# The first layer's spatial product as seven block products, with sums formed behind the turning

## The chip, the cores and the metric

The kernel runs on one core of a Trainium2 chip. The core has a matrix engine (TensorE; PE in the profile, with its weight loads as PEld), three elementwise engines (VectorE, DVE; ScalarE, ACT; GpSimd, POOL), and a sequencer (SyncE, SP) whose queue issues all of this kernel's transfers. The metric is the device time of one execution in microseconds (us): the median of several executions.

## The reference, cut to what matters

The program computes two attention layers and two gated MLP layers in turn, on x of 2048 rows (S) by 640 columns (D), and the change concerns the first MLP layer:

```python
z = gelu(layernorm(x) @ w_in)                  # 2048 x 1728
z1, z2 = z[:, :864], layernorm(z[:, 864:])
g = w_sp @ z2 + b_sp[:, None]                  # w_sp is 2048 x 2048: the spatial product
x = x + (z1 * g) @ w_out                       # w_out is 864 x 640
```

Both MLP layers use the same w_sp, w_in and w_out, and both attention layers the same q, k, v and o weights. To keep precision with 16-bit operands, every matrix is split in a high and a low half (float16 each), and a product is three: high by high, high by low, low by high.

## The kernel before, in words

Each layer runs in three stages. Attention (`phase1a`, class `Attention`) writes o to DRAM; `phase1b` makes x1, z1 and z2 for 16 tiles t of 128 rows; and the third stage multiplies by w_sp, gates, and multiplies by w_out.

The third stage of the first layer (`phase2`) goes through the 16 row tiles t of w_sp. The rows of tile t are fetched (`rows`, 1 MB), their largest absolute value gives a power-of-two scale (`scale`: one reduction over 2048 columns and five instructions on one column, DVE), the scaled rows are split into halves (`split`: high on ACT, low on DVE), and both 128x1024 column halves are turned by a DMA transpose into `wt` (from the staging tile `wn`). `product` is 96 matmuls per row tile: 16 blocks of 128 by three half products by two column halves of 432. `gate` adds the bias and multiplies by z1 (ACT, DVE), scales and splits the result, and turns it (`ut`); `tail` multiplies it by w_out, 42 matmuls of 320 columns into the two-bank PSUM tile `yp`, of which there is one. The tail of tile t-1 runs behind product t. `early` normalises the new x rows for the next attention. Three quarters of the turned `wt` are stored to DRAM (`store`, `g.turned`) for the second layer.

The third stage of the second layer (`phase2s`) already uses seven block products, as Winograd's form of Strassen's method does: w_sp and z2 are taken as 2x2 blocks (even and odd row tiles, even and odd column tiles of w_sp; the left and right 432 columns of z2), so that a pair p of row tiles costs 7 block products of 24 matmuls each and not 8. The seven combinations of z2 blocks, `zb[0]` to `zb[6]`, are made by `blocks` in `phase1b` (ACT, DVE and POOL). Of the seven combinations of w_sp, three are read back from `g.turned`, and four (S1 to S4) are formed by DVE from scaled rows (scaled by ACT with the scales that the first layer kept) and then turned.

In the third stages the order on PE, SP, DVE and ACT is the order of the code (`manual_schedule(engines=ALLE)`); only POOL's is left to the scheduler. An engine runs its instructions in that order, and one that waits holds up all behind it.

## Time and profile before

| what | value |
|---|---|
| median of 3 executions | 2226.51 us (2224.16 to 2227.24) |
| profiled execution | 2220.46 us, span 2218.7 us |
| first layer: attention, phase1b, third stage (with the next attention's first units) | 0 to 592, 592 to 784, 784 to about 1190 us |
| second layer: attention, phase1b, third stage | to 1690, 1690 to 1877, 1877 to 2219 us |
| busy over the span | PE 95%, DVE 66%, ACT 53%, POOL 42% |

PE is busy nearly all of the time, so a stage is as long as its matmuls where nothing makes PE wait. A row of the table by stage gives, for each engine, busy us and instructions in that stretch, then the granted TensorE clock, the busy share of the DMA engines and GB/s. A row of the timeline gives start, duration, engine, line, operation and tiles, and in brackets the idle time before it and what ended it. `SPq` rows are the issuing of a transfer, not its landing.

### The profile page before, as it was taken

What the parts mean: (1) busy time and instruction counts of PE and PEld (TensorE: products, weight loads), DVE (VectorE), ACT (ScalarE), POOL (GpSimd) and SP (SyncE); (2) the same over time, 40 slices, a digit from 0 to 9 for tenths busy, and PEclk for the clock granted to TensorE, in tenths of its full rate; (3) what the DMA queues carried; (4) which work ended last, traced back from release to release, by engine and by line L of the source; (5) the groups of instructions that cost most, each with busy time, mean ns of one, the idle gap of its engine ahead of it and who ended that gap; (6) DMA issues with size and microseconds to landing.
All of it is one profiled execution on the core that took longest, in us unless ns stands there. A gap on an engine that the chain in (4) does not pass through costs nothing. (4 is left out here: it accounts for less than half of the span.)

```text
span 2218.7 us, 48917 instructions
## 1 busy us (share of the span) xinstructions
PE 2102.8 (95%) x19917; PEld 1269.7 (57%) x19917; DVE 1466.5 (66%) x2804; ACT 1177.0 (53%) x1415; POOL 934.3 (42%) x625
## 2 busy tenths in 40 slices
PE   4889899999899999999999999999989999999999
PEld 2455565666555555555655556666665555555555
DVE  8678888787654654554445787887776667465455
ACT  3499888887632332221222998888875334223321
POOL 2399988888310101000000888788874223000000
PEclk9999999999999999999999999999999999999999
DMA  5624635356746678977655344344566334977875
GB/s 170 181 71 128 142 98 137 106 138 157 177 122 175 165 197 220 248 201 209 187 136 142 93 110 120 105 114 111 147 186 178 100 107 128 251 197 200 225 209 134
DMA packets 515202, 345.03 MB, mean 156 GB/s; under 512 B 409952, under 2 KB 452960, under 8 KB 510624
## 3 DMA queue, kind: packets, MB, share of 16 engines
q1 hardware_dynamic: 514976, 341.90, 59.0%
q8 instruction: 156, 2.56, 0.5%
q14 instruction: 70, 0.57, 0.1%
HBM read 152.53 MB, written 101.20 MB: 114 GB/s over the span
## 5 line engine op out<-in xcount | busy, mean ns | idle before, releaser
L1431 POOL TENSOR_TENSOR PHL<-P,PHL 128x1024 f16<-128x1024 f32 x310 | 658.8, 2133 | 170.6 <-ACT PHL L1430 121.7
L1412 ACT ACTIVATE P<-es,sc 128x1024 f32<-128x1024 f32 x320 | 356.1, 1113 | 85.0 <-PE es L1376 82.1
L1422 DVE TENSOR_REDUCE mx<-mp 128x2 f32<-128x1024 f32 (+2 forms) x384 | 320.9, 861 | 85.6 <-PE mp L1376 84.6
L1430 ACT CAST PHL<-P 128x1024 f16<-128x1024 f32 x320 | 333.5, 1042 | 6.3
L279 POOL TENSOR_TENSOR lnrs<-lnve,mhalf 128x1 f32<-128x1 f32 x92 | 56.4, 620 | 664.2 <-DVE lnve L278 613.8
L375 PEld LDWEIGHTS <-th 128*128 128x128 f16 x1920 | 187.5, 98 | 164.4 <-DMA th<-xnhl 2.6
L757 PE MATMUL gp<-zh,wt 128*128 128x432 f16 x1024 | 231.3, 346 | 0.0
L757 PEld LDWEIGHTS <-wt 128*128 128x128 f16 x1536 | 150.2, 98 | 129.0
L1465 PEld LDWEIGHTS <-PHL 128*128 128x128 f16 x5120 | 167.0, 96 | 52.4 <-DVE oat L1486 13.8
L543 PEld LDWEIGHTS <-wt 128*128 128x128 f16 x1344 | 131.3, 98 | 113.5 <-DMA wt<-wn 1.0
L1465 PE MATMUL pv<-vs,PHL 128*128 128x41 f16 x5120 | 172.6, 182 | 15.6 <-DVE oat L1486 10.8
L375 PE MATMUL zp<-wi,th 128*128 128x432 f16 x960 | 180.5, 346 | 1.9 <-DMA th<-xnhl 1.3
L1176 PE MATMUL vps<-wvh,xt 128*128 128x320 f16 x640 | 157.3, 305 | 11.3 <-DVE vs L1182 5.8
L1405 PEld LDWEIGHTS <-qk 60*128 60x128 f16 (+1 forms) x2048 | 76.7, 94 | 151.0 <-issue 106.1
L1405 PE MATMUL mp<-qk 60*128 60x512 f16 (+3 forms) x1024 | 127.1, 306 | 30.7 <-DVE mx L1422 24.2
L757 PE MATMUL gp<-zl,wt 128*128 128x432 f16 x512 | 135.4, 346 | 0.0
L1405 PE MATMUL es<-qk 64*128 64x256 f16 (+3 forms) x1024 | 124.1, 299 | 11.4 <-ACT P L1412 8.6
L1232 PE MATMUL qps<-xt,wqh 128*128 128x512 f16 x380 | 121.3, 380 | 0.0
L1208 PE MATMUL yps<-wo,o 128*128 128x320 f16 x720 | 119.8, 303 | 1.2 <-DMA o<-o 1.2
L1176 PEld LDWEIGHTS <-xt 128*128 128x128 f16 x960 | 87.7, 100 | 45.6 <-issue 13.7
L770 DVE TENSOR_TENSOR u<-u,cz 128x864 f32<-128x864 f32 x16 | 16.9, 1059 | 144.2 <-ACT u L768 136.6
L1232 PE MATMUL kps<-xt,wkh 128*128 128x512 f16 x340 | 106.8, 379 | 0.6 <-DVE phl L1273 0.4
(276 smaller groups left out, 3935.5 us busy)
## 6 DMA issues: line engine op xcount, KB each, us to landing
wr<-in_B_w_sp_dram SPq DMA_DIRECT2D x32, 1024.0 KB
qk<-st SPq DMA_DIRECT2D x256, 120.0 KB
z<-z SPq DMA_DIRECT2D x32, 432.0 KB
cz<-z SPq DMA_DIRECT2D x32, 432.0 KB
turned<-wt SPq DMA_DIRECT2D x24, 512.0 KB
wt<-turned SPq DMA_DIRECT2D x24, 512.0 KB
st<-qhl SPq DMA_DIRECT2D x40, 256.0 KB
st<-khl SPq DMA_DIRECT2D x40, 256.0 KB
```

Source lines behind the costliest of these rows:

```text
L375: nc.tensor.matmul(zp[:, n, :FHH], a[:, k, :], b[:, k, c:c + FHH], start=(k == 0 and j == 0), stop=(k == KD - 1 and j == 2))
L543: nc.tensor.matmul(o[:, :FHH], wt[:, x, m, :], zb[b][:, y, m, :], start=start and i == j == 0, stop=i == NP - 1 and j == 2, skip_group_che ...
L757: nc.tensor.matmul(gp[:, n, :FHH], ready[t][:, k % 2, a, k // 2, :], b[:, k, n * FHH:(n + 1) * FHH], start=(i == 0 and j == 0), stop=(i == ...
L1176: nc.tensor.matmul(ps, a[:, k, c], b[:, k, n * 320:(n + 1) * 320], start=(i == 0), stop=(i == 14))
L1208: nc.tensor.matmul(ps, a[:, k, :], b[:, k, c], start=(i == 0), stop=(i == 14))
L1232: nc.tensor.matmul(ps, a[:, k, c], b[:, k, :], start=(i == 0), stop=(i == 14))
L1405: nc.tensor.matmul(out[:, h, o:o + w], a[r, ac], b[r, bc], start=o == 0, stop=False, skip_group_check=True)
L1412: self.last_of["ACT"] = nc.scalar.activation(self.Pf[t], es, AF.Exp, scale=g.esc).ins
L1422: self.last_of["DVE"] = nc.vector.tensor_reduce(mx[:, e, :, i], mp[:, :, o:o + w], AX.X, ALU.max).ins
L1430: nc.scalar.copy(hl[:, 0], P)
L1431: (nc.gpsimd if t < self.T - self.TAIL or t % 2 == 0 else nc.vector).tensor_tensor(hl[:, 1], P, hl[:, 0], ALU.subtract)
L1465: nc.tensor.matmul(pv[:, i, h, 0:PVC - 1], self.P[u][:, x, h, o:o + 128], v[:, j, h0 + h, :], start=first and h == x == 0 and (u, o, i, j) ...
```

## The change

The first layer's third stage is now `phase2f`, and takes the same seven block products per pair of row tiles as the second layer's. `phase1b` makes the seven blocks of z2 in both layers (`whole` is gone). What is different from `phase2s` is how the combinations of w_sp come about: all four quarters of a row pair are scaled, split and turned as before (`split`, `turn`), then POOL adds the turned halves up to float32 again (`back`, into the tiles `f0`, `f1`, `f2`), DVE forms S1 to S4 from these (`mix`), and ACT and DVE split each sum into halves (`high`, `low`) straight into the tile that PE reads. There are two staging tiles `wn` and eight `wt` tiles, reused between the quarters and the sums (`place`). The statistics of `early` and its normalising are two steps now.

The seven blocks need more memory than the two tiles before. So the attention weights q, k, v lie where blocks 0, 3, 4 of z will be, and the turned x where block 1 will be and in the place of w_in's and w_out's halves (`g.w0`); the attention weights are stored to DRAM in the first attention (`g.wkept`), and read again behind the last products of the stage. Therefore the next attention's first units and its values, which stood between products 10 to 15, come after the last product, and the attention's pools are opened there (`nxt.sbuf`, `nxt.psum`). The last two tails stand among those units. The first half of w_in is loaded in the background of attention in both layers.

```diff
+def phase2f(g, w_sp, x1_d, z1_d, zb, out, nxt, rest):
...
+    def place(p, b):
+        tag = {"11": "a", "21": "c", "S2": "c", "12": "d", "S3": "e", "S4": "g", "22": f"x{p % 2}", "S1": f"x{1 - p % 2}"}[b]
+        wt[p, b] = (pt0 if tag in ("a", "x0", "c") else pt1).tile([128, 2, NP, 128], F16, tag="wt" + tag, name="wt")
+        return wt[p, b]
...
+    def back(t, i, tag):
+        if t < NT:
+            o = wt[t // 2, f"{t % 2 + 1}{i + 1}"]
+            f[tag] = pf.tile([128, NP, 128], F32, tag=tag, name=tag)
+            nc.gpsimd.tensor_tensor(f[tag], o[:, 0], o[:, 1], ALU.add)
+
+    def mix(o, a, b, op):
+        nc.vector.tensor_tensor(f[o], f[a], f[b], op)
+
+    def high(p, b, tag):
+        if p < NP:
+            nc.scalar.copy(place(p, b)[:, 0], f[tag])
+
+    def low(p, b, tag):
+        if p < NP:
+            nc.vector.tensor_tensor(wt[p, b][:, 1], f[tag], wt[p, b][:, 0], ALU.subtract)
...
+        product(pa, p, "11", 0)
...
+        split(r0, 0)
+        turn(r0, 0)
+        scaled(v, pa, t)
+        scaled(v1, pa, t + 1)
...
+        split(r1, 1)
...
+        product(pc, p, "S1", 3)
+        turn(r1, 1)
+        store(r0, 0)
...
+        back(r0, 0, "f0")
+        split(r1, 0)
...
+        product(pb, p, "S2", 4)
+        turn(r1, 0)
+        rows(r1 + 2)
+        back(r1, 1, "f2")
+        plus(qq, pb, t, v)
+        plus(u[:, FHH:], pc, t, qq)
+        split(r0, 1)
...
+        store(r1, 1)
+        rows(r0 + 2)
+        if pend:
+            now.append(nxt.early(*tail(*pend.pop(0))))
...
+        product(pa, p, "12", 1, False)
+        turn(r0, 1)
+        back(r1, 0, "f1")
+        scaled(u[:, :FHH], pa, t)
+        if not last:
+            mix("f2", "f1", "f2", ALU.add)
+            mix("f1", "f0", "f1", ALU.subtract)
+            mix("f0", "f2", "f0", ALU.subtract)
+            high(q, "S2", "f0")
+            low(q, "S2", "f0")
...
+        if pend:
+            now = [nxt.early(*tail(*pend.pop(0)))]
...
+        product(pb, p, "S3", 5, False)
+        plus(q1, pb, t + 1, v1)
+        plus(u1[:, FHH:], pc, t + 1, q1)
+        high(q, "S3", "f1")
+        low(q, "S3", "f1")
+        store(r0, 1)
+        back(r0, 1, "f1")
...
+        scale(r1 + 2)
...
+        product(pd, p, "22", 6)
+        high(q, "S1", "f2")
+        plus(u1[:, :FHH], pd, t + 1, q1)
+        low(q, "S1", "f2")
...
+        pend.append((*gate(t + 1, u1, z1[0]), x1[0]))
+        if not last:
+            mix("f1", "f1", "f0", ALU.subtract)
...
+        product(pe, p, "S4", 2)
+        high(q, "S4", "f1")
+        plus(u[:, FHH:], pe, t, u[:, FHH:])
+        low(q, "S4", "f1")
+        pend.append((*gate(t, u, z1[1]), x1[1]))
+        scale(r0 + 2)
...
+    nxt.kept_back = []
+    for m in range(2):
+        for nm in "qk":
+            run(nxt.unit(0, m, {nm: bank("abcd"[2 * m + (nm == "k")])[:, :L]}))
+            if nm == "qk"[m == 0]:
+                tail(*pend.pop(0))
+    sb.close()
+    rest.close()
+    nxt.sbuf()
...
```

Two places show how the order moves. The first is DVE in the middle of the first layer's third stage. In a row, `wn` is the staging tile, `wr` a row tile of w_sp, `xo` or `cx` the new rows of x, `q` and `u` the 432-column pieces of g, `f_` the float32 sums, `wt` the turned tile that PE reads. Before, behind one row tile's scale:

```order
L793 SCALAR_TENSOR_TENSOR xo<-cyp,xs,cx_13308 128x640
L745 SCALAR_TENSOR_TENSOR wn<-wr,wiv,wn 128x1024 x2
L276 BN_STATS lnst<-xo 128x6 x2
L277 BN_AGGR lnmv<-lnst 128x2
L278 TENSOR_SCALAR lnve<-lnmv 128x1
L285 TENSOR_SCALAR xt<-xo,lnmv,lnrs 128x640
L770 TENSOR_TENSOR u<-u,cz_13709 128x864
```

The change, behind the scale of the even row tile of a pair:

```order
L742 SCALAR_TENSOR_TENSOR wn<-wr,wiv,wn 128x1024 x3
L786 SCALAR_TENSOR_TENSOR q<-gb,unt,v 128x432
L786 SCALAR_TENSOR_TENSOR u<-gc,unt,q 128x432
L742 SCALAR_TENSOR_TENSOR wn<-wr,wiv,wn 128x1024
L816 SCALAR_TENSOR_TENSOR cx_13259<-cyp,xs,cx_13259 128x640
L292 BN_STATS lnst<-cx_13259 128x6 x2
L293 BN_AGGR lnmv<-lnst 128x2
L294 TENSOR_SCALAR lnve<-lnmv 128x1
L765 TENSOR_TENSOR f_13439<-f_13529,f_13439 128x1024
L765 TENSOR_TENSOR f_13529<-f_13406,f_13529 128x1024
L765 TENSOR_TENSOR f_13406<-f_13439,f_13406 128x1024
L773 TENSOR_TENSOR wt<-f_13406,wt 128x1024
```

The instruction that empties the tail's PSUM tile (L793 before, L816 now) stood ahead of the splits of the next row tile and now stands behind all four splits of the next pair; the sums follow it.

The second place is SP's queue over the same stretch. Before, for one row tile:

```order
L746 DMA_TRANSPOSE wt<-wn 128x16x128 x2
L763 DMA cz_13709<-z_0_6 128x864
L722 DMA wr<-in_B_w_sp_dram 128x2048
L763 DMA cx_13713<-x_0_6 128x640
L750 DMA turned_0<-wt 128x2048
L750 DMA turned_1<-wt 128x2048
L1133 DMA xn<-xnhl 128x1280
```

The change, for one pair, from the fetches of z1 on:

```order
L790 DMA cz_13332<-z_0_4 128x864
L752 DMA_TRANSPOSE wt<-wn 128x16x128 x2
L756 DMA turned_0<-wt 128x2048
L752 DMA_TRANSPOSE wt<-wn 128x16x128
L717 DMA wr<-in_B_w_sp_dram 128x2048
L756 DMA turned_1<-wt 128x2048
L717 DMA wr<-in_B_w_sp_dram 128x2048
L817 DMA x_3<-cx_13259 128x640
L752 DMA_TRANSPOSE wt<-wn 128x16x128
```

Where both staging tiles of a row tile were filled and turned together, the third and the fourth transpose of a pair now stand apart, each behind a store that waits for an earlier transpose to land, and the staging tile of the third is that of the first.

More of the change, by code (lines that the diff above doesn't have):

```diff
@@ L151, in place, with load @@
         return self.h, self.l
-    def load(self, stage, width=864, tag="wst", keep=True, ahead=0):
+    def load(self, stage, width=D, tags=(), keep=True, ahead=0):
         nc = self.g.nc
@@ L398, in phase1b @@
             th = xn_t(xn)
[L399 to L405 removed]
+        more = other_scales(g, wm, (g.wu,), 6, 0, 0) if first else iter(())
         for i, t in enumerate(ts):
```

517 lines of the change are left out of this document (290 added, 227 removed).

## The prediction

> **What bounds the kernel now.** I read the table by stage first, for the first layer's third stage, two pairs of row tiles inside the third stages of both layers, and the last 67 us of the second layer's phase1b.
>
> ```profile
> 784.00:1206.00 422.00, 417.91 (x2494) 241.72 (x2493) 201.50 (x365) 97.11 (x111) 32.75 (x36) 1.00 0.75 198
> ...
> 875.00:922.00 47.00, 47.00 (x281) 27.27 (x280) 24.34 (x45) 10.54 (x11) 3.90 (x4) 1.00 0.95 252
> ...
> 1962.00:2004.00 42.00, 42.00 (x253) 24.61 (x252) 21.92 (x33) 11.32 (x11) 0.00 (x0) 1.00 0.81 212
> ...
> 1810.00:1840.00 30.00, 29.54 (x164) 15.69 (x162) 21.46 (x38) 14.88 (x18) 9.05 (x9) 1.00 0.40 116
> 1840.00:1877.00 37.00, 36.34 (x200) 19.31 (x199) 27.27 (x48) 13.45 (x20) 12.44 (x12) 1.00 0.45 106
> ```
>
> Columns are PE, PEld, DVE, ACT and POOL busy, clock, DMA share, GB/s. In the third stages PE never idles and DVE (third figure) is busy half of the time. So PE sets the length, and seven products for eight would be worth their matmuls, as long as DVE stays below PE. The timeline gives the sizes: PE of the second layer (a block product of 24 matmuls every 4.38 us), then DVE of the first layer's third stage over one row tile.
>
> ```profile
> 1900.00 4.54 PE L543 MATMUL gd<-zb,wt 128*128 128x432 f16 x24
> ...
> 1904.38 4.54 PE L543 MATMUL ge<-zb,wt 128*128 128x432 f16 x24
> ```
>
> ```profile
> 982.76 1.06 DVE L770 TENSOR_TENSOR u<-u,cz 128x864 f32<-128x864 f32 x1 [8.91 <-ACT u L768]
> ...
> 986.80 1.12 DVE L780 SCALAR_TENSOR_TENSOR un<-u,uiv,un 128x864 f16<-128x864 f32 x1 [1.01 <-ACT un L778]
> 987.83 2.28 DVE L728 TENSOR_REDUCE am<-wr 128x1 f32<-128x2048 f32 x1
> ...
> 990.85 0.88 DVE L793 SCALAR_TENSOR_TENSOR xo<-cyp,xs,cx 128x640 f32<-128x640 f32 x1
> 992.09 2.48 DVE L745 SCALAR_TENSOR_TENSOR wn<-wr,wiv,wn 128x1024 f16<-128x1024 f32 x2 [0.36 <-ACT wn L744]
> 994.49 0.88 DVE L276 BATCH_NORM_STATS2 lnst<-xo 128x6 f32<-128x320 f32 x2
> ...
> 996.46 0.61 DVE L285 TENSOR_SCALAR xt<-xo,lnmv,lnrs 128x640 f32<-128x640 f32 x1 [0.67 <-POOL lnrs L279]
> 1005.99 1.06 DVE L770 TENSOR_TENSOR u<-u,cz 128x864 f32<-128x864 f32 x1 [8.91 <-ACT u L768]
> ```
>
> The period is 1005.99 - 982.76 = 23.23 us; four products are 17.52, so a tail is 5.71. DVE stands idle for 8.91 us of it. From the same rows: a gate holds DVE for 5.07 us (982.76 to 987.83, with 1.01 of waiting for ACT), a scale 3.02 (to 990.85), a tail's last step 0.88, statistics 1.3 (994.49 to the reciprocal root on POOL), normalising 0.61, a low half of a split 1.24.
>
> **The change part by part.** Added on DVE per pair of row tiles are four sums, four low halves of sums, and five additions out of PSUM; on ACT high halves of sums and the smaller first terms. The second layer has them (by line and shape):
>
> ```profile
> L515 DVE TENSOR_TENSOR s<-s,wr 128x1024 f32<-128x1024 f32 x7 | 8.6, 1225 | 5.4 <-ACT wr L499 4.8
> L527 DVE TENSOR_TENSOR wn<-s,wn 128x1024 f16<-128x1024 f32 x14 | 17.0, 1218 | 0.0
> L550 DVE SCALAR_TENSOR_TENSOR q<-gb,unt,v 128x432 f32<-128x432 f32 x16 | 10.6, 662 | 12.0 <-PE gb L543 12.0
> L522 ACT CAST wn<-s 128x1024 f16<-128x1024 f32 x14 | 14.6, 1044 | 47.9 <-DVE s L515 47.9
> L547 ACT ACTIVATE v<-ga,bsp,unt 128x432 f32<-128x432 f32 x16 | 10.4, 697 | 1.2 <-PE ga L543 1.2
> L744 ACT ACTIVATE wn<-wr,wiv 128x1024 f16<-128x1024 f32 x28 | 30.6, 1140 | 41.4 <-DVE wiv L732 41.4
> ```
>
> *Matmuls.* Eight block products fewer: 8 x 4.38 = 35.0 us. A pair costs PE 7 x 4.38 + 2 x 5.71 = 42.1 us instead of 46.5.
>
> *DVE's sum.* Two scales 6.0, four low halves of splits 5.0, four sums 4.9, four low halves of sums 4.9, five additions 3.4, two gates 10.1, two tails with their normalisation 5.6: 39.9 us of PE's 42.1. Nothing is left for waiting, and DVE's queue is strictly in order. So waits decide.
>
> *The turning.* From the issue of a transpose, or the end of DVE's low half right before it, to PE as the waiting reader of the turned tile (timeline, second layer; the third pair of rows under a full DMA queue):
>
> ```profile
> 1817.70 1.65 SPq L293 DMA_TRANSPOSE th<-xnhl  x1
> 1821.72 5.65 PE L375 MATMUL zp<-wi,th 128*128 128x432 f16 x30 [0.46 <-DMA th<-xnhl]
> ```
>
> ```profile
> 2203.88 1.12 DVE L569 SCALAR_TENSOR_TENSOR un<-u,uiv,un 128x864 f16<-128x864 f32 x1 [1.01 <-ACT un L567]
> ...
> 2209.62 3.03 PE L575 MATMUL ga<-w,ut 128*128 128x320 f16 x21 [0.41 <-DMA ut<-un]
> ```
>
> ```profile
> 1886.18 7.36 SPq L536 DMA_TRANSPOSE wt<-wn  x1
> ...
> 1895.61 4.55 PE L543 MATMUL gb<-zb,wt 128*128 128x432 f16 x24 [0.61 <-DMA wt<-wn]
> ```
>
> Ten blocks took 4.0 us, fourteen 4.6, so sixteen about 4.9 (estimate); 9.4 when the queue was full. Between these I take 4.9, since the quarters of one pair are turned one at a time behind light traffic. The Trainium skill, "DMA: Bandwidth & Descriptors", section "Latency and other measured facts", gives DMA transposes 261 GB/s, which makes 512 KB 2.0 us; the sum of the stage would by that be near the third rival's below, about no change. The rows here disagree with it as a landing time: 4.6 us for 448 KB.
>
> *POOL's additions.* The trace has none from two halves; the nearest row has the same size. Below it, POOL and DVE in the second layer's phase1b:
>
> ```profile
> L1431 POOL TENSOR_TENSOR PHL<-P,PHL 128x1024 f16<-128x1024 f32 x310 | 658.8, 2133 | 170.6 <-ACT PHL L1430 121.7
> ```
>
> ```profile
> L446 DVE TENSOR_TENSOR zb<-z,zb 128x432 f16<-128x432 f32 x23 | 26.5, 1177 | 4.3 <-ACT zb L445 4.3
> ...
> L446 DVE TENSOR_TENSOR zb<-zt,zb 128x432 f16<-128x432 f32 x29 | 18.2, 660 | 2.4 <-ACT zb L445 2.3
> ```
>
> I take 2.1 us for one. The second pair shows one and the same DVE form at 660 ns, and at 1177 where POOL subtracts at the time: DVE with two SBUF tensors stands still while POOL works. Bounds for this: 0, and all four additions, 8.5 us per pair.
>
> *One cycle of DVE*, from the end of the even tile's scale. Low half of r0's left quarter at 2.4 (ACT's high half first, 1.14). ACT then has the two first terms (1.4), so the second low half ends at 4.9. The third waits for a staging tile: the first transpose lands at 7.3, ACT takes until 8.4, but POOL's addition has begun at 7.3 and DVE gets through at 9.4; ends 10.7. Two additions, 12.1. POOL's second addition goes first, so the fourth low half ends at 14.1. Now DVE empties the tail: 15.0, statistics 16.3. The third transpose was issued at 10.7, landed at 15.6, was added by 17.7; only then come three sums (21.4), S2's high half on ACT, its low half (23.7), normalising, second tail and statistics (26.5), two additions (27.9), S3's low half and normalising (29.7), a scale (32.7), an addition and S1's low half (34.6), a gate (39.7), a sum, an addition and S4's low half (42.8), a gate (47.9), a scale: **50.9 us**, against 46.5 for a pair before. PE follows: the second tail needs the one PSUM tile that DVE empties at 15.0, so PE's pair ends at 15.0 + 5.7 + 3 x 4.38 = 33.8 in DVE's cycle.
>
> *Sum of the stage.* Its start: in the second layer DVE is done with z2 4.3 us after PE's first product (below), here a scale lies between, 7.3. The first pair has no tails or normalisation (-5.6) but the split of w_out (seven pieces of 0.88, 6.2); S4's sum falls in a wait: DVE ends it at about 58.
>
> ```profile
> 1877.31 4.54 PE L543 MATMUL ga<-zb,wt 128*128 128x432 f16 x24
> ...
> 1879.07 2.54 DVE L446 TENSOR_TENSOR zb<-zt,zb 128x432 f16<-128x432 f32 x3
> ...
> L91 DVE SCALAR_TENSOR_TENSOR wul<-wst,iv,wuh 128x640 f16<-128x640 f32 x6 | 5.2, 884 | 10.5 <-ACT wuh L90 10.5
> ```
>
> Then five cycles (254.5), PE's 33.8 to the end of the seventh pair, a last pair at PE's own 42.1 (nothing is left to prepare), and two tails, 11.4: 399.8. Before: 16 x 23.23 = 371.7. The stage becomes **28 us longer** where PE alone would make it 35 shorter.
>
> *phase1b of the first layer.* Blocks instead of two halves: the second layer's does that with PE hardly waiting. But the preparation behind its last tiles is heavier: in its last 67 us DVE is busy 21.46 + 27.27 = 48.7; the second layer's preparation in it (four sums, two low halves, 7.3) goes, four scales, four low halves, three sums and one more low half (22) come: 63 of 67. I charge 3 us, bounds 0 and 8.
>
> *The end of the stage.* Values and units come later, with no product to hide their ACT and DVE steps, but values now follow the units and hide the trip of q and k through DRAM. Before, PE loses 6.0 us there:
>
> ```profile
> 1180.00:1206.00 26.00, 21.91 (x144) 12.01 (x143) 11.97 (x17) 4.96 (x9) 0.69 (x1) 0.97 0.83 198
> 1206.00:1230.00 24.00, 22.09 (x198) 12.37 (x196) 17.97 (x28) 11.34 (x18) 4.21 (x2) 0.96 0.51 108
> ```
>
> I take no difference, bounds -5 and +6. The weights' extra 10 MB go out and come in where the DMA has room: nothing, for the reload starts three products and more ahead of its reader.
>
> Sum: 28 + 3 = **+31 us**: 2220.5 becomes 2251.5 for the profiled execution, and 2226.5 becomes 2257.5, say 2258, for the median, which lies 6 us above the profile.
>
> **The rivals.**
> - *Landing hidden.* Transposes land in time and POOL blocks nothing; DVE's own order still holds. Then the third and fourth low halves end at 6.2 and 8.9, sums start at 11.1, and a cycle is 44.3. The same sum (first pair, five cycles, PE's offset, last pair with two tails) is 52 + 221.5 + 28.6 + 53.5 = 355.6, 16 less than before; 2213 with phase1b. Faster, and it decides from a cycle of about 45 downwards. Against it: both waits are in the order, with 4.0 us as the shortest landing seen.
> - *PE bound.* DVE runs ahead of PE throughout: -35, 2191. Against it: 39.9 of 42.1 us without one handover to ACT.
> - *Landing in 2.4 us.* From ten to fourteen blocks the landing grew by 0.6 us, which makes 2.4 for sixteen without a fixed part; POOL still blocks. The cycle is then 47.1 and the sum 375: about +3, with phase1b 2232, and no change where POOL blocks little. By the 261 GB/s of the Trainium skill ("DMA: Bandwidth & Descriptors", the same section) the kernel would end here too.
> - *Queue full.* Rows, stores and fetches of z1 lie before the transposes, and a landing takes 7 us (between 4.9 and 9.4): the cycle is 55.1, the stage 425, +53 by the same sum; 2282.
>
> **How the numbers follow.** Forecast 0.60, landing hidden 0.12, PE bound 0.05, landing in 2.4 us 0.08, queue full 0.15. Its own range: landings from 4.0 with nothing blocked (cycle 48.2, stage 381, +10) to 6 us (+44): 2236 to 2272. The range over all reaches to the hidden landing and to the full queue: 2212 to 2288. A difference of 0.2% is 4.5 us, about what this kernel's measurement can tell. Faster: 0.12 + 0.05 and half of the short landing, 0.21; slower: 0.60 + 0.15 less its lower edge, 0.72; same 0.07.
>
> **What would show it.** In the changed kernel's stage DVE busy near 40 us in a pair that lasts about 51; PE idle before the second tail (released by DVE's step that empties PSUM), and DVE idle before the third low half and before the first sum (released by ACT behind a transpose, and by POOL). Rows of the forms above should keep their durations; two-tensor ones on DVE should lengthen beside POOL's additions. I am wrong if PE has no idle time in pairs two to seven, if DVE's cycle is under 46, or if the loss lies in phase1b or at the stage's end instead.

## The result, and the profile of the changed kernel

The changed kernel takes 2290.07 us (median of 4 runs, 2288.22 to 2294.76) where the kernel before takes 2225.34 us beside it: a ratio of 1.0295, 95% interval 1.0274 to 1.0315. It is slower, as forecast, but by 65 us and not by 31. Its profiled execution took 2288.59 us against 2220.46 us, 68.1 us more.

Where they went, by the start times in TensorE's timelines of the two kernels (layer 1 up to the last row):

| stretch | before | after | difference | forecast |
|---|---|---|---|---|
| up to the first product of phase1b | 591.9 | 595.3 | +3.4 | 0 |
| phase1b | 191.8 | 200.2 | +8.4 | +3 (0 to 8) |
| third stage, block products and tails | 371.7 | 423.1 | +51.4 | +28 |
| units, values, up to the first score of layer 2 | 40.4 | 50.9 | +10.5 | 0 (-5 to +6) |
| the rest (layer 2) | | | -5.6 | 0 |

The third stage first. TensorE's timeline of the changed kernel over one pair, from the second tail of one to that of the next; in brackets the time it stood idle and who released it:

```profile
1040.50 8.31 PE L813 MATMUL cyp<-w,ut 128*128 128x320 f16 x42 [6.93 <-DVE cx L816]
1048.65 4.54 PE L779 MATMUL gb<-zb,wt 128*128 128x432 f16 x24
...
1074.93 5.87 PE L813 MATMUL cyp<-w,ut 128*128 128x320 f16 x42
1080.64 4.55 PE L779 MATMUL ga<-zb,wt 128*128 128x432 f16 x24
1092.14 8.09 PE L813 MATMUL cyp<-w,ut 128*128 128x320 f16 x42 [6.96 <-DVE cx L816]
```

The pair lasts 1092.14 - 1040.50 = 51.6 us. The second tail waits 7 us for the step that empties the one PSUM tile, the place the forecast named. And behind such a wait the same 42 matmuls take 8.1 to 8.3 us instead of 5.87. Now DVE and ACT around the first of these waits:

```profile
1034.52 2.07 DVE L742 SCALAR_TENSOR_TENSOR wn<-wr,wiv,wn 128x1024 f16<-128x1024 f32 x1 [3.84 <-ACT wn L741]
1039.57 0.87 DVE L816 SCALAR_TENSOR_TENSOR cx<-cyp,xs,cx 128x640 f32<-128x640 f32 x1
1043.20 3.74 DVE L765 TENSOR_TENSOR f<-f,f 128x1024 f32<-128x1024 f32 x3 [1.41 <-POOL f L762]
```

```profile
1033.34 1.15 ACT L741 ACTIVATE wn<-wr,wiv 128x1024 f16<-128x1024 f32 x1 [3.98 <-DMA wt<-wn]
```

The third low half waits for ACT, ACT for a transpose to leave its staging tile, and the sums wait for POOL: what the forecast laid out. The groups by line for the whole stage, then for phase1b (busy, mean of one, idle time before them and who ended it):

```profile
L813 PE MATMUL cyp<-w,ut 128*128 128x320 f16 (+1 forms) x672 | 109.3, 328 | 53.4 <-DVE cx L816 44.4 <-ACT w L90 4.1 <-DVE w L91 4.0
L779 PE MATMUL gb<-zb,wt 128*128 128x432 f16 x384 | 74.9, 353 | 7.6 <-DVE q L786 7.6
...
L384 PE MATMUL zp<-wi,th 128*128 128x432 f16 x480 | 91.8, 350 | 6.7 <-DMA th<-xnhl 6.7
```

44.4 us in six waits are the second tails. The others stand in the first two pairs (w_out's halves 8.1, q 7.6) and in phase1b (6.7 for the turned normalised rows), and the forecast named none of them. At the end of the stage, the values (PE), and ACT, which copies their results out of PSUM (`vs`):

```profile
1231.63 2.20 PE L1345 MATMUL vps<-zb,zb 128*128 128x320 f16 x15
1235.63 2.20 PE L1345 MATMUL vps<-zb,zb 128*128 128x320 f16 x15 [1.80 <-DVE phl L1442]
1244.62 15.16 PE L1345 MATMUL vps<-zb,zb 128*128 128x320 f16 x90 [6.79 <-DVE vs L1351]
```

```profile
1239.26 0.60 ACT L1421 ACTIVATE khl<-gd 128x512 f16<-128x512 f32 x1 [3.17 <-DMA pk<-phl]
...
1243.29 0.77 ACT L1350 ACTIVATE vs<-vps 128x320 f16<-128x320 f32 x2
```

ACT copies the values out only at 1243.29, behind the outputs of the units; of these one waits 3.17 us for a store.

Busy time by window (PE, PEld, DVE, ACT, POOL, granted clock, DMA share, GB/s): one pair, and the end. Where TensorE stands and starts again the mean clock is below 1.

```profile
1010.00:1062.00 52.00, 45.07 (x256) 25.76 (x255) 38.69 (x60) 13.94 (x15) 13.06 (x8) 0.93 0.67 186
...
1232.00:1260.00 28.00, 19.41 (x121) 12.68 (x120) 7.68 (x14) 6.25 (x13) 0.00 (x0) 0.82 0.71 179
```

### The profile page after: what moved, and what is told of

Its sections match the earlier page's. It is cut to its first block, busy times and chain, and to the rows that moved or that the text cites. A ratio compares the mean times of both kernels' runs of the same rounds, so it can differ in the third digit from the quotient of the medians.

```text
span 2286.8 us, 48875 instructions
## 1 busy us (share of the span) xinstructions
PE 2098.4 (92%) x19725; PEld 1259.0 (55%) x19725; DVE 1619.0 (71%) x2951; ACT 1221.1 (53%) x1490; POOL 1054.3 (46%) x690
## 4 chain that ended last, share of the span: by engine, by line
PE 63%; DVE 13%; DMA 8%; ACT 8%; issue 5%; POOL 2%; SPq 1%; ACTq 0%; DVEq 0%; POOLq 0%
PE zp L384 12%; PE cyp L813 4%; PE cyp L586 3%; PE vps L1345 3%; PE pv L1634 3%; PE gb L537 3%; PE ga L537 3%; PE qps L1401 3%; DMA wt<-wn 3%; ACT P L1581 3%; PE mp L1574 3%; PE yps L1377 3%; PE gb L779 2%; PE kps L1401 2%; PE es L1574 2%
## 5 line engine op out<-in xcount | busy, mean ns | idle before, releaser
L384 PE MATMUL zp<-w,th 128*128 128x432 f16 x960 | 180.4, 346 | 0.0
L762 POOL TENSOR_TENSOR f<-wt 128x1024 f32<-128x1024 f16 x32 | 74.5, 2330 | 229.5 <-DMA wt<-wn 194.1
L1401 PEld LDWEIGHTS <-zb 128*128 128x128 f16 x1200 | 103.7, 100 | 102.9 <-issue 11.9
L813 PE MATMUL cyp<-w,ut 128*128 128x320 f16 (+1 forms) x672 | 109.3, 328 | 53.4 <-DVE cx L816 44.4
L1574 PEld LDWEIGHTS <-qk 64*128 64x128 f16 (+1 forms) x1728 | 65.9, 93 | 127.1 <-issue 94.3
L1574 PE MATMUL mp<-qk 60*128 60x512 f16 (+3 forms) x864 | 108.3, 305 | 17.3 <-DVE mx L1591 11.5
L813 PEld LDWEIGHTS <-ut 128*128 128x128 f16 (+1 forms) x672 | 71.0, 106 | 91.8 <-issue 55.1
L1574 PE MATMUL es<-qk 64*128 64x256 f16 (+3 forms) x864 | 106.3, 299 | 9.5 <-ACT P L1581 7.3
L1345 PE MATMUL vps<-zb,zb 128*128 128x320 f16 x480 | 77.1, 311 | 15.9 <-DVE vs L1351 12.8
L769 ACT CAST wt<-f 128x1024 f16<-128x1024 f32 x32 | 33.3, 1044 | 105.5 <-DVE f L765 88.8
```

The costliest lines, as they stand in the source:

```text
L384: nc.tensor.matmul(zp[:, n, :FHH], a[:, k, :], b[:, k, c:c + FHH], start=(k == 0 and j == 0), stop=(k == KD - 1 and j == 2))
L813: nc.tensor.matmul(yp[:, n, :320], a[:kn[k], k, :], b[:kn[k], k, n * 320:(n + 1) * 320], start=(k == 0 and j == 0), stop=(k == KO - 1 and ...
L1401: nc.tensor.matmul(ps, a[:, k, c], b[:, k, :], start=(i == 0), stop=(i == 14))
L1574: nc.tensor.matmul(out[:, h, o:o + w], a[r, ac], b[r, bc], start=o == 0, stop=False, skip_group_check=True)
```

## The experiments

All start from the changed kernel. "Pair" is the time from one second tail to the next, mean of the three pairs behind the one in which w_out is stored (two row tiles of the kernel before: 46.5). "Second pair" is the start of the second pair's second tail after the start of the stage. "End" runs from the last tail's end to the first score of layer 2.

| kernel | time, us | pair | second pair | end |
|---|---|---|---|---|
| changed | 2290.1 | 51.7 | 85.9 | 41.0 |
| e1_reduce | 2290.5 | 51.8 | 84.0 | 39.5 |
| e2_order | 2289.3 | 50.1 | 84.2 | 39.9 |
| e3_staging | 2274.7 | 49.0 | 80.6 | 41.0 |
| e4_back | 2280.6 | 49.8 | 84.0 | 39.8 |
| e5_z1_reduce | 2277.8 | 49.3 | 81.7 | 40.8 |
| e6_queue | 2288.6 | 50.6 | 82.4 | 41.0 |
| e7_queue_reduce | 2279.0 | 49.4 | 80.6 | 39.6 |
| e8_wout_end | 2290.4 | 51.6 | 74.4 | 47.6 |
| e9_stores_late | 2265.9 | 47.5 | 77.2 | 39.9 |
| e10_fill | 2252.4 | 45.1 | 78.5 | 39.6 |
| e11_mended | 2243.3 | 45.4 | 73.8 | 35.4 |
| e12_places | 2241.9 | 44.2 | 75.6 | 39.0 |
| e13_places2 | 2230.1 | 44.2 | 68.7 | 36.9 |
| e14_places3 | 2217.1 | 44.1 | 68.7 | 30.5 |

e1 to e10 are one execution each; the stretches, read inside one trace, tell more there than the total. The kernel before took 2218 to 2224 us beside them.

**Is VectorE's work the bound? (e1)**

```diff
-            nc.vector.tensor_reduce(am, raw[t], AX.X, ALU.max, apply_absolute_value=True)
+            nc.vector.tensor_reduce(am, raw[t][:, :128], AX.X, ALU.max, apply_absolute_value=True)
```

> Leaves out: the maximum of each row of the spatial weights is taken over the first 128 of its 2048 columns in layer 1's third stage, so the row's scale may differ; everything that follows is unchanged. Theory (VectorE's ordered cycle sets the pair): the reduction falls from 2.28 us to about 0.25 us, twice in a cycle, so a pair goes from 51.5 us to about 47.4 us; over six cycles some -24 us in the stage, and the time near 2264 us. Rival (the tail's PSUM tile or the landing of the transpositions sets the pair): the reductions lie in idle time, the pair stays within 0.5 us of 51.5 us and the time within 5 us of 2290 us.

The theory fell: 4 us less of DVE's work in each pair (two reductions of 2.28 us became two of 0.28), and the pair lasts 51.8 us. DVE's timeline of one pair of e1_reduce, and SyncE's at its start:

```profile
1073.91 1.28 DVE L742 SCALAR_TENSOR_TENSOR wn<-wr,wiv,wn 128x1024 f16<-128x1024 f32 x1 [1.15 <-ACT wn L741]
...
1083.25 2.07 DVE L742 SCALAR_TENSOR_TENSOR wn<-wr,wiv,wn 128x1024 f16<-128x1024 f32 x1 [5.83 <-ACT wn L741]
...
1091.93 3.74 DVE L765 TENSOR_TENSOR f<-f,f 128x1024 f32<-128x1024 f32 x3 [1.40 <-POOL f L762]
```

```profile
1073.38 1.57 SPq L790 DMA_DIRECT2D cz<-z  x2
1075.25 6.90 SPq L752 DMA_TRANSPOSE wt<-wn  x2
```

```profile
1082.07 1.15 ACT L741 ACTIVATE wn<-wr,wiv 128x1024 f16<-128x1024 f32 x1 [5.96 <-DMA wt<-wn]
```

DVE reaches the third low half earlier and stands 5.83 us there instead of 3.84. The first transpose of the pair is issued at 1075.25 and ACT is let go at 1082.07: 6.8 us, against 4.9 in the changed kernel (there from 1080.12 to 1084.98). The two z1 fetches (864 KB) are issued on the same queue just before it; with DVE faster they stand closer ahead. About half of the time saved on DVE, 2.0 of 4.0 us, became this wait for the landing. The rest went in smaller waits, for PE's products (gb 1.36 us instead of 1.00, gd 0.33 instead of none) and for ACT (0.41 instead of none), and in a low half of 1.99 us instead of 1.21. The Trainium skill, "DMA: Bandwidth & Descriptors", section "Queues, rings and completion order", says that each DMA engine takes the descriptors of a ring in order; a landing that takes longer with 864 KB issued just ahead fits that.

**Is it the PSUM tile? (e2)**

```diff
+        if pend:
+            now.append(nxt.early(*tail(*pend.pop(0))))
         split(r0, 1)
...
-        if pend:
-            now.append(nxt.early(*tail(*pend.pop(0))))
```

> The first tail of a pair is written ahead of the fourth quarter's split, so VectorE empties its PSUM tile before it forms that low half. Theory (VectorE's cycle sets the pair): the same work in another order, the pair stays within 1 us of 51.5 us, the second tail's wait is shorter and as much is waited for elsewhere, the time within 6 us of 2290 us. Rival (the late emptying of the single PSUM tile is the cause): the 7 us that the second tail waits for it in each pair go, 44 us in all, and the time is near 2246 us.

50.1 us: 1.6 of the 7 us came back, not 7, and the second tail still waits more than 5 us. That is a little more than the 1 us that the theory allowed, so the order of these two steps is worth something; but the wait of the second tail is mostly a symptom, and the rival with its 7 us is out.

**Staging tiles and POOL (e3, e4)**

```diff
-    pr, ph, pf = pool("fr", 2), pool("fh", 2), pool("ff", 1)
+    pr, ph, pf = pool("fr", 2), pool("fh", 3), pool("ff", 1)
...
-        v, v1, qq, q1 = [vec(nm) for nm in ("v", "v1", "q", "q1")]
+        qq, q1 = [vec(nm) for nm in ("q", "q1")]
```

> A third staging tile for the halves ahead of the turning (two tiles of 432 columns are given up for it, v and q being one tile now). Theory: the wait of about 4 us for a landing (ScalarE's third high half, VectorE behind it) leaves the cycle, the sums begin as much earlier, and the pair goes from 51.5 us to about 47.5 us; -24 us in the stage, the time near 2266 us. Rival (VectorE's 39.9 us of work and POOL's additions hold the sums back anyway): the wait moves to the sums, the pair stays above 50.5 us and the time within 6 us of 2290 us.

```diff
-            nc.gpsimd.tensor_tensor(f[tag], o[:, 0], o[:, 1], ALU.add)
+            nc.gpsimd.tensor_copy(f[tag], o[:, 0])
```

> Leaves out: the sums are formed from the turned high halves alone (POOL copies the high half into float32 and does not add the low one). Theory: POOL's operation falls from 2.33 us to somewhere between 0.9 and 1.5 us, VectorE's low halves beside it from 2.0 us to 1.6 us or less, the sums begin about 1 us earlier; in all 2 to 3 us of a pair, -12 to -18 us in the stage, the time near 2275 us. Rival (POOL's additions lie in waits that are there anyway): the pair stays within 0.5 us of 51.5 us and the time within 5 us of 2290 us.

Both gained, between theory and rival: 2.7 us a pair with the third tile (4 expected), 1.9 with the shorter operation (2 to 3 expected). So the waits for landing and POOL's additions are in the loop, while shortening DVE's reductions alone gained nothing. In e4_back the gain is not POOL's alone: its operation falls from 2.33 to 1.04 us, and the two low halves of DVE that ran beside it fall from 2.07 and 1.87 to 1.28 us. What ate the rest in e3_staging stands in SyncE's order and at the sums:

```profile
1066.78 4.78 SPq L752 DMA_TRANSPOSE wt<-wn  x2
1071.64 0.89 SPq L756 DMA_DIRECT2D turned<-wt  x1
1072.64 3.49 SPq L752 DMA_TRANSPOSE wt<-wn  x1
```

```profile
1080.23 3.74 DVE L765 TENSOR_TENSOR f<-f,f 128x1024 f32<-128x1024 f32 x3 [3.58 <-POOL f L762]
```

The third transpose's low half was ready at 1070.1, but a store stands ahead of it in SyncE's queue and waits for the first transpose to land. The sums wait 3.58 us instead of 1.41: the wait has moved there.

**The queue (e5, e6, e7, e9)**

e5 takes the z1 fetches away from the first transpose and keeps the shorter reductions of e1 on DVE:

```diff
         turn(r0, 1)
+        if p:
+            z1 = [fetch("z1", z1_d[i]) for i in (t + 1, t)]
...
-            z1 = [fetch("z1", z1_d[i]) for i in (t + 3, t + 2)]
```

> Leaves out, as e1_reduce: a row's maximum is taken over 128 of its 2048 columns. And the two fetches of z1 for the next pair (864 KB) are issued in the next pair behind its last turning instead of just ahead of its first. New theory (the pair is a loop through the landing of the transpositions: low half, turning, landing, POOL's addition, sums, then the sums' consumers; VectorE's work counts only where it lies in that loop): in e1_reduce the first turning landed 6.8 us after its issue, in the changed kernel 4.9 us, because the fetches now stood right ahead of it; with them out of the way it lands in about 4.9 us or less, and the pair goes from 51.5 us to about 49.5 us, -12 us in the stage, near 2279 us. Rival (TensorE's own chain from the second tail to the next pair took the saved reductions): the landing is shorter but the pair stays within 0.5 us of 51.5 us.

49.3 us, as the new theory said. In the trace of e5_z1_reduce the first transpose of a pair is issued at 1114.77 and ACT is let go at 1120.05: 5.3 us, between the 4.9 of the changed kernel and the 6.8 of e1_reduce. Beside e1_reduce the new place of the fetches is worth 2.5 us a pair. What it is worth with whole reductions was not run, so the 2.4 us against the changed kernel cannot be divided between the two edits. e6 puts the moved fetches together with the third tile, and e7 adds the shorter reductions:

```diff
         turn(r1, 1)
-        store(r0, 0)
...
         turn(r1, 0)
+        store(r0, 0)
         rows(r1 + 2)
```

> The third staging tile of e3_staging, and in SyncE's order the first store goes behind the third turning and the z1 fetches behind the fourth. Theory (loop through the landings): in e3_staging the third turning was issued 2.5 us after its low half, because the store ahead of it waited for the first landing; now it is issued at once, the sums begin 2.5 us earlier or more, and the pair goes from 49.0 us to about 46 us; -18 us against e3_staging, the time near 2257 us. Rival (VectorE's own 39.9 us with its handovers now set the pair): 48.5 us or more, the time near 2272 us.

> As e6_queue, and the row's maximum over 128 of 2048 columns (left out: the rest of the row). Theory: once the landings no longer set the pair, VectorE's order does, and the 4.1 us of reductions count: 2 to 4 us less per pair than e6_queue, near TensorE's 42 to 43 us, -12 to -24 us against e6_queue. Rival (the landings or POOL's additions still set it): within 0.7 us of e6_queue's pair.

The sums did begin earlier, 13.1 us after the first low half (16.1 in the changed kernel, 14.8 in e3_staging), and yet the pair was longer than e3_staging's. SyncE and ACT of e6_queue, later in a pair:

```profile
1087.85 11.03 SPq L752 DMA_TRANSPOSE wt<-wn  x1
1098.93 1.05 SPq L790 DMA_DIRECT2D cz<-z  x2
1100.07 0.38 SPq L1292 DMA_DIRECT2D xn<-xnhl  x1
```

```profile
1105.49 0.72 ACT L1289 CAST xnhl<-xt 128x640 f16<-128x640 f32 x1 [8.48 <-DMA xn<-xnhl]
```

The fourth transpose waits for its place until 1098.9, and behind it the z1 fetches, which I had put there, and the store of the normalised rows; ACT waits 8.48 us for that store, and the high half that it owes PE's next product comes behind. I had moved the obstacle from one loop into another. e7's 1.2 us against e6 are for that reason no clear answer. e9 instead puts the stores where SyncE waits for the gates anyway:

```diff
-        store(r1, 1)
         rows(r0 + 2)
...
         x1 = [fetch("x1", x1_d[i]) for i in (t + 1, t)]
+        store(r0, 0)
+        store(r1, 1)
+        store(r0, 1)
```

> The third staging tile, and SyncE's order changed otherwise than in e6_queue: the three stores of turned halves go behind the fetches of x1, where SyncE waits for the gates anyway, and the z1 fetches between the two fetches of rows. Theory (a pair is a loop through SyncE's one ordered queue: what is issued between a low half and its turning, or between the fourth turning and the store of the normalised rows, is in the loop): the sums begin about 13 us after the first low half, as in e6_queue, and ScalarE no longer waits 8.5 us for the normalised rows' store, so the pair is about 46.5 us; the time near 2258 us. Rival (the transfers' bytes and not their order set it): the waits only move, 48.5 us or more, near 2272 us.

47.5 us lies halfway between the theory (46.5) and the rival (48.5), and 2265.9 us nearer to the rival's 2272 than to the theory's 2258. The theory gave the way and not the size. No transfer was removed, so the 1.5 us over e3_staging come from order on the one queue, and not from fewer bytes.

**Handovers (e10)**

```diff
         nc.vector.tensor_scalar(xs, pw, g.pw[:, 6:7], 2.0 ** -28, ALU.mult, ALU.mult)
+        fill()
         nc.vector.scalar_tensor_tensor(hl_u[:, 1, :FH], u, iv, hl_u[:, 0, :FH], ALU.mult, ALU.subtract)
...
-        pend.append((*gate(t, u, z1[1]), x1[1]))
-        scale(r0 + 2)
+        pend.append((*gate(t, u, z1[1], lambda: scale(r0 + 2)), x1[1]))
```

> As e9_stores_late, and the scale of the next row and one sum are written between a gate's high half (ScalarE) and its low half (VectorE), so that VectorE does not stand still there. Theory: three handovers of about 1 us leave VectorE's order, now in the loop; 2 to 3 us less per pair than e9_stores_late, 43.5 to 44.5 us. Rival (VectorE has slack, as e1_reduce showed for the changed kernel): within 0.5 us of e9_stores_late's pair.

45.1 us: 2.4 less than e9, in the 2 to 3 us expected, though from e9's 47.5 that ends above the 43.5 to 44.5. Here a shorter order of DVE counts, where in e1, with the landings as they were, 4 us less work were nothing.

**The terms outside the pair (e8, e11 to e14)**

e8 leaves out w_out's splits and tries another place for the values (an empty iterator for the splits; each unit's output ahead of two halves of the values, in the stage's own banks):

```diff
-    wu = staged()
+    wu = iter(())
...
+    for t, nm in enumerate(("ea", "be", "ca", "db")):
+        todo[t]()
+        run(nxt.value(t, nm, bank))
```

> Two changes in separate places, read separately. Left out: w_out's seven fetches and splits in the first pair (w_in's left half is multiplied in their place). And behind the last tail the values' products are put into the banks of the stage itself, one output of the units ahead of each two halves, instead of behind all of the outputs in attention's own banks. Theory: the second tail of the second pair begins 13 us earlier against the start of the stage (85.9 us now, about 73 us then); and the stretch from the last tail's end to the first score falls from 41.0 us to about 33 us. Rival (the first pairs wait for the turned halves and not for w_out; the values wait for outputs, not for banks): less than 4 us in either place. The time near 2290 - 13 - 8 = 2269 us by the theory.

The second pair's second tail begins 74.4 us into the stage instead of 85.9: 11.5 us are w_out's chain. The end became 6.6 us longer: the banks I gave to the values were those of the units' keys, so the products waited for the very outputs they were to overtake. PE of e8_wout_end:

```profile
1232.60 4.16 PE L1344 MATMUL gb<-zb,zb 128*128 128x320 f16 x15 [6.75 <-DVE phl L1441]
...
1250.28 4.04 PE L1344 MATMUL gd<-zb,zb 128*128 128x320 f16 x15 [5.33 <-DVE phl L1441]
```

e11 to e14 leave nothing out. e11 is e10 with w_out's pieces fetched ahead and the values in free banks:

```diff
+            q, tag = ((nxt.e1, "xh"), (nxt.e2, "xt"), (p2, "x1"), (p2, "x1"))[k % 4 if k < 6 else 0]
+            st = q.tile([128, D], F32, tag=tag, name="wst")[:n]
...
+        for step in ("ffff", "sf", "sf", "s", "ssf", "s", "s"):
...
+        yp = py.tile([128, 2, 512], F32, tag="yp", name="vyp") if t % 2 == 0 else None
+        run(nxt.value(t, (bank("e"), bank("a")) if t % 2 else (yp[:, 0], yp[:, 1])))
```

> As e10_fill, and: w_out's first four pieces are fetched ahead of the first pair into four tiles (the two places of x1 among them), so that its splits never wait for a fetch; and the values' products go into the output product's and one more bank of the stage, in turn with the units' outputs, two products ahead of them. Theory: against e10_fill about 10 us less up to the second pair's second tail, and from the last tail's end to the first score 41 us becomes about 36 us; in all 2290 - 35 (pairs) - 10 - 5 = about 2238 us, still not faster than the kernel before. Rival: the pieces of w_out displace the first turned halves on SyncE's queue and the gain in the first pair stays under 4 us; 2248 us or more.

4.7 us in the first pairs (10 expected; the rival's mechanism was there, the fourth transpose now landed behind the fetches) and 4.2 us at the end; 2243.3 us, ratio 1.0104 (1.0083 to 1.0126). e12 moves five things:

```diff
-        if p == 2:
+        if p == NP - 2:
             g.wu.keep()
...
+        if pend:
+            now.append(nxt.early(*tail(*pend.pop(0))))
         split(r0, 1)
...
+    with behind("x13"):
+        back(1, 1, "f2")
+        back(1, 0, "f1")
```

> As e11_mended, with five edits, each read at its own place of the trace. (1) In the stage before (layer 1's output projection and first product), POOL's three additions of turned halves, and the sums behind them, wait until VectorE has formed the low half of the normalised rows of that step and of the next. Theory: those additions doubled VectorE's own durations at 750 us and made TensorE wait 7.4 us for the turned rows; the stage falls from about 200 us to 193 to 195 us. Rival (the transposition's landing is late for another reason): the 7 us of waiting stay. (2) w_out's split halves are stored in the last pair but one and not in the third: the pair that took 51 us instead of 45 us takes 46 us or less. (3) w_out's first four fetches are issued ahead of z1's: in the first pair the 6.3 us that TensorE waits for q fall to 3 us or less. (4) The first tail of a pair is emptied ahead of the fourth quarter's split and (5) the normalising stands between a sum's high and its low half: TensorE's 2.3 us of waiting in each pair go, 42 to 43.5 us a pair. In all -7 - 5 - 4 - 10 against 2243 us: about 2217 us, level with the kernel before. Rival (one of the waits takes the place of another, as so far in two experiments): above 2232 us.

The pair is at 44.2 us and the third pair's extra 5 us are gone, but the whole gained 1.4 us. PE of e12_places, in phase1b and right behind the last pair (a unit's product):

```profile
757.93 8.34 PE L384 MATMUL zp<-wi,th 128*128 128x432 f16 x30 [4.38 <-DMA th<-xnhl]
...
1158.94 5.28 PE L1415 MATMUL ga<-zb,zb 128*128 128x512 f16 x15 [5.83 <-DMA zb<-xn]
```

w_out's stores, put ahead of the last pair, now made its transposes late by as much as they had cost in the third; and w_out's and z1's fetches pushed the fourth transpose of the first pair back (6.55 us of waiting). In phase1b the edit had moved the sums on DVE that follow POOL's additions, and the wait that stands there in e11_mended, 1.97 us, fell to 0.29; POOL's first two additions stayed where they were, and with them a wait of 4.38 (5.09 in e11_mended). e13 moves these, too:

```diff
+    with behind("p12"):
+        back(1, 1, "f2")
+        back(1, 0, "f1")
...
+    turn(0, 1)
     wu = staged()
...
+    g.wu.keep()
     run = lambda it: [None for _ in it]
```

> As e12_places, with what its trace showed amiss mended in three places, each read by itself. (1) In the stage before, the first two of POOL's additions stayed where they were in e12_places (748.1 us, right ahead of VectorE's slow differences), and TensorE's wait of 4.4 us at 757.9 us stayed with them, while the wait at 785 us, whose sums had moved, fell from 2.9 to 0.3 us. Now the two additions stand behind the next step's difference on POOL, the third behind the difference after. Theory (the additions hold VectorE, which is late with the normalised rows): the 4.4 us go too, under 1 us is left of 5.9 us, and the first product of the third stage starts near 789 us. Rival (that wait has another cause): it stays above 3 us. (2) w_out's halves are stored behind the last pair instead of between the last two, where they pushed 8 us of waiting into the last pair and 3.6 us behind it: the stretch from the second tail of the last pair but one to the last tail's end falls from 59.1 us to about 51 us (42.4 us in e11_mended, at another place of the cut), and the end by 3 us. (3) In the first pair the fourth turning is issued ahead of w_out's and z1's fetches: TensorE's 6.6 us of waiting for it fall to 2 us or less. In all some -16 us: about 2226 us, level with the kernel before or up to 0.3 per cent above it. Rival (the pieces only move): above 2234 us.

2230.1 us, ratio 1.004 (1.0026 to 1.0054). The last pair and the first got what was expected. In phase1b the theory fell halfway. DVE of e12_places and then of e13_places2, the same two subtractions:

```profile
748.26 4.97 DVE L441 TENSOR_TENSOR zb<-zt,zb 128x432 f16<-128x432 f32 x2
```

```profile
747.07 1.12 DVE L441 TENSOR_TENSOR zb<-zt,zb 128x432 f16<-128x432 f32 x2
748.10 0.81 DVE L308 TENSOR_TENSOR xnhl<-x,xnhl 128x640 f16<-128x640 f32 x1
```

So POOL's additions did hold DVE: 4.97 us against 1.12 for the same work. (The Trainium skill, "SBUF — State Buffer", section "Who interferes with whom", has the rule: a DVE instruction with two SBUF inputs contends with a POOL instruction that reads SBUF, and the ports that the two share are an exclusive lock. The rows agree.) But PE still waited 4.58 us at 756.93, since the turning landed late. SyncE of e13_places2:

```profile
747.34 0.56 SPq L757 DMA_DIRECT2D turned<-wt  x1
747.96 0.42 SPq L718 DMA_DIRECT2D wr<-in_B_w_sp_dram  x1
748.49 0.82 SPq L398 DMA_DIRECT2D z<-z  x1
749.42 1.71 SPq L309 DMA_TRANSPOSE th<-xnhl  x1
```

1.9 MB were issued within 2 us ahead of it, and it landed 7.5 us after its issue. Two causes stood one behind the other; taking the first away showed the second. e14 takes that away:

```diff
         turn(1, 0)
+    with behind("s12"):
         store(1, 1)
         rows(3)
...
-        for step in ("ff", "ffs", "fs", "fs", "ssf", "s", "s"):
+        for step in ("ff", "ff", "", "sfsf", "ss", "sf", "s", "s"):
...
+        run(nxt.value(t, lambda n: bank("eya"[(2 * t + n) % 3]) if (2 * t + n) % 3 != 1 else py.tile([128, 2, 512], F32, tag="yp", name="vyp")[:, 0]))
```

> As e13_places2, with three edits read each at its place. (1) In e13_places2 POOL's additions had moved, the low half of the normalised rows was ready 6 us earlier, and TensorE still waited 4.6 us: their turning was issued at 749.4 us and landed at 756.9 us, 7.5 us later, behind a store of 512 KB, rows of 1024 KB and z1's 432 KB issued within the 2 us before. Now that store and those rows are issued behind it. Theory (the bytes ahead of a turning on the one queue set its landing): the wait falls from 4.6 us to under 1 us. Rival (something else delays the landing): above 3 us. (2) In the first pair the sum S4 and w_out's splits are written behind the second output row's parts, so that VectorE takes TensorE's result q 3 to 5 us earlier: the wait of 5.9 us falls to 2 us or less. (3) The values' products use three separate banks in turn, since two halves of one tile waited for each other: the waits of 3.5 us between them go. In all -4 - 4 - 3 = about 2219 us, 0.1 per cent below the kernel before to 0.3 per cent above it. Rival (the waits only move on): 2227 us or more.

2217.1 us (12 runs, 2210.76 to 2224.17) against 2223.7 us of the kernel before (17 runs): ratio 0.9973, 95% interval 0.9961 to 0.9986. With the same arithmetic, products and transfers as the changed kernel, 73 us less. PE of e14_places3 in phase1b, in the first pair and over a pair in the middle:

```profile
755.47 5.65 PE L384 MATMUL zp<-wi,th 128*128 128x432 f16 x30
...
767.16 5.65 PE L384 MATMUL zp<-wi,th 128*128 128x432 f16 x30 [0.57 <-DMA th<-xnhl]
...
836.30 7.09 PE L781 MATMUL gc<-zb,wt 128*128 128x432 f16 x22 [5.78 <-DVE wt L775]
...
1078.31 5.87 PE L816 MATMUL cyp<-w,ut 128*128 128x320 f16 x42 [1.09 <-DVE cx L819]
```

```profile
1020.00:1064.00 44.00, 42.46 (x254) 24.53 (x252) 36.71 (x59) 13.54 (x15) 13.52 (x8) 1.00 0.75 215
```

The wait in phase1b is gone, the end is 30.5 us. In the first pair the rival held: the wait for q went, and 3.90 + 5.78 = 9.7 us appeared further on, before gc. In a pair in the middle PE is busy 42.46 of 44 us at full clock. The total met its forecast (2219) partly by luck: the first pair gave none of the 4 us forecast for it (68.7 us in both kernels), phase1b 4.2 of 4, and the end 6.4 where 3 were forecast.

## Why the prediction was right or wrong

- *PE no longer sets the length, waits do; slower.* Right in sign and in place. The layout named the wait of the second tail, that of the third low half and that of the sums, and the trace has all three (6.93, 3.84, 1.41 us).
- *One cycle of DVE, 50.9 us.* Measured 51.7 (mean of three pairs), and not by luck: in the rows of one cycle, counted from the end of the even tile's scale, the third low half ends at 10.6 (laid out: 10.7), the tail is emptied at 14.5 (15.0), the sums begin at 17.3 (17.7) and the cycle ends at 51.4. The landing taken as 4.9 us (estimate from 4.0 and 4.6) is 4.9 in the trace; POOL's addition taken as 2.1 is 2.33 in the mean; the low half beside it 2.07 instead of 1.28.
- *"Nothing is left for waiting", 39.9 us of DVE's work as the reason.* Wrong as a reason, and the size hid that. e1 took a tenth of DVE's work away and got nothing. The loop that closes the pair goes low half, SyncE's queue, landing, POOL's addition, sums, and DVE's order is in it only in part: e3 and e9 shorten it at the queue, e4 at POOL (and at DVE's low halves beside it), and behind these e10 gains 2.4 us from DVE's order.
- *Sum of the stage.* Here is the step that failed. It put the first pair at 58 us and the second tail of the second pair 15.0 us behind, 73.0 us into the stage; measured 85.9, +12.9. I had counted w_out's seven splits as 6.2 us of DVE's time and nothing else. They are a chain (fetch behind other fetches on the queue, ACT, DVE, two staging tiles) with PE's first tails at its end; e8 puts it at 11.5 us, 5.3 more than charged. The other 7.6 us are there in e8_wout_end, too: 74.4, where the sum without w_out's 6.2 gives 66.8. In that kernel's first pair, rows of DVE, then of ACT and of PE:

```profile
810.78 2.13 DVE L742 SCALAR_TENSOR_TENSOR wn<-wr,wiv,wn 128x1024 f16<-128x1024 f32 x1 [5.16 <-ACT wn L741]
812.84 1.21 DVE L765 TENSOR_TENSOR f<-f,f 128x1024 f32<-128x1024 f32 x1
815.16 2.17 DVE L773 TENSOR_TENSOR wt<-f,wt 128x1024 f16<-128x1024 f32 x1 [1.11 <-ACT wt L769]
```

```profile
809.60 1.15 ACT L741 ACTIVATE wn<-wr,wiv 128x1024 f16<-128x1024 f32 x1 [4.09 <-DMA wt<-wn]
```

```profile
819.16 6.90 PE L779 MATMUL gb<-zb,wt 128*128 128x432 f16 x24 [4.98 <-DVE q L786]
```

The second low half of the pair waits 5.16 us for ACT and so for a landing, which the cycle of a pair charges at the third low half only. And S4's sum with its low half, which I took to fall in a wait, stands in DVE's order for 4.5 us (812.84 to 817.33) while PE waits for q. No run removes either alone, so how the 7.6 us divide between them is not shown; in e14, which writes S4 later, the wait for q goes and others take its place.

The next five pairs are 7.7 us longer than five cycles. The third pair of the stage, with w_out's 2.2 MB of stores on the queue, lasts 56.6 and makes 5 of the 7.7; e12, which moves these stores, has 43.9 there. At the stage's end the seventh pair's second tail takes 7.93 us instead of 5.87, 2.1 longer than charged, and 0.6 is a wait for the turned gates. In all 12.9 + 7.7 + 2.1 + 0.6 = 23.3 us: 399.8 forecast, 423.1 measured.
- *phase1b, +3 with bounds 0 and 8.* Measured 8.4, just above the upper bound. I had compared busy times (63 of 67 us); what hurt were POOL's additions on DVE's subtractions and a store with rows ahead of a turning (e12, e13, e14), both of them waits and not work. Moving these brought the stage from 200.2 to 194.0 us; the last 2.2 us against the kernel before are left open.
- *The end of the stage, no difference.* Measured +10.5. The step charged the values as if they ran while q and k go through DRAM. But their outputs queue on ACT and DVE behind the units' outputs, which wait for their own stores, and their two PSUM banks fill at once (the rows at the end of the stage, above). Other banks and another order took 10.5 us off this stretch (41.0 to 30.5).
- *Rivals.* "Queue full" (2282, chance 0.15) came nearest in time, though not by a landing of 7 us in each pair; its mechanism showed in e1 and in phase1b. "Landing hidden" needed a cycle of 44.3, and that is what e12 to e14 reach, by rearrangement.
- Not explained: the 3.4 us by which phase1b starts later, for which no run was made (in e13_places2 and e14_places3 it starts at 593.3 and 595.1), and the 5.6 us that layer 2 gains, 4.8 of them ahead of its third stage.

## What to carry to other kernels

When work moves from PE to a chain over DVE, POOL and a transpose, do not add up the busy time of the fullest engine: find the loop, with the DMA queue's order as a link of it, and count on it what each instruction waits behind. Remove one link's work to see if it is in the loop at all; a link that gains nothing today (e1) may be worth something when another is loosened (e5, e10). And charge one-time work such as a weight's preparation as a chain with a reader at its end, not as busy time.

## What the runs showed of the hardware

TensorE is slow after a wait of a few microseconds. Two rows, of e4_back and of e3_staging:

```profile
808.87 6.24 PE L779 MATMUL ga<-zb,wt 128*128 128x432 f16 x24 [2.07 <-DMA wt<-wn]
```

```profile
1026.12 5.87 PE L813 MATMUL cyp<-w,ut 128*128 128x320 f16 x42 [3.55 <-DVE cx L816]
```

In the groups of 15 and more matmuls of phase1b and the third stage of layer 1, in the changed kernel and all experiments, no wait of up to 2.06 us slowed the matmuls behind it. From 2.07 to 3.55 us it went both ways: 6.24 us instead of 4.54 in the first row, nothing in the second, 7.53 instead of 5.87 after 2.26 us in e10_fill. From 3.56 us on they were slower in every row, by 1.3 to 2.9 us: 42 of them took 8.31 us instead of 5.87 after 6.93 us, 24 took 7.34 instead of 4.54 after 5.87 us (e13_places2, first pair). The granted clock says the same: 0.50 in the 2 us behind the first row's wait (809 to 811), 1.00 around the second (1022 to 1032); 0.93 over a pair with a wait of 7 us, 1.00 over one without. The Trainium skill, "TensorE: Matmul & The Clock Gate", section "Part 1: The HAM clock gate (the "warmup" mystery)", gives a free-running window of 3.4 us after which an idle array runs at half clock. That no sharp limit shows here fits a window that does not start with the wait; that 2.07 us were once enough, less than one such window, no run here explains.
